# Last batch of a Fourier stage: spectra kept in SBUF, its inverse blocks moved, logits in groups of six and two batches

## The chip, the cores and the metric

One core of a Trainium2 chip. The metric is the device time of one launch in microseconds (us), as the median of three runs. A 0.2% difference is 2.9 us.

## What is computed

Two layers in a row. The first is a filter in the frequency domain, the second a mixture of experts with a greedy, global assignment of tokens:

```python
X = np.fft.rfft(x, axis=1)                 # x: 8 batches x 2496 x 256, float32
y = np.fft.irfft(X * (filt_r + 1j * filt_i)[None], n=2496, axis=1)
t = y.reshape(19968, 256)
logits = t @ w_gate                        # 19968 x 8
order = np.argsort(-logits.flatten())      # best pairs first
# go through order: a token takes its expert unless it has one, or the expert has 2496 already
for e in range(8):
    out[mask_e] = np.maximum(t[mask_e] @ w1[e], 0) @ w2[e]
```

## The kernel before

The length 2496 is taken as 39 x 64, and the program has three stages on one core.

**Fourier stage** (`Fft.run`). It is written as a table of events; each has a slot (ten slots a batch) and a priority, and a scheduler then lays the instructions of each engine in one fixed order. For a batch b the steps are: `s1` (first transform), `s2` (second transform, ten blocks of TensorE matmuls; DVE multiplies each with the filter F into P and Q, POOL combines them; the ten results P are the batch's spectra), `tr` (ten blocks q: four transposes of spectra into PSUM, then `split` into a high part yh on ACT and a low part yl on DVE), `inv1` (first inverse transform of block q: six matmuls over two rows of 256, a copy of PSUM into a tile zt, and two DMA stores of zt, 128 KB each, into the HBM buffer zd of the batch). zt has four buffers (ZB). `inv2` is the second inverse transform: a unit loads 600 KB of zd as a tile z, and its rows go to xs in HBM.

The logits don't wait for the inverse transform. They are computed from the spectra: gate matmuls on P (in `tr`), a transpose (`trv`) with a split into Vh and Vl, `v1` (an inverse transform for the logits alone, five groups g), a copy of its result on ACT, `v2` (22 transposes and a copy), `v3` (a matmul and a copy into lg), and `Route.prep` (seven DVE instructions over lg). Batches 0 to 6 go through v1, v2, v3 and prep together, batch 7 alone behind them. When its prep is done, the first round of the expert threshold starts.

**Routing and the remaining units** (`emit`). 30 units of inv2 remain when the logits are done. They are woven by hand, in one TensorE order, with the eleven threshold rounds (`Route.threshold`; a round is eleven to thirteen count matmuls `rt<-A,Gm` of L569, a few short DVE steps, one matmul L582, a few DVE steps). Blocks q = 0 and 1 of batch 7 stand among its own steps, q = 2 to 4 right behind its v3, and q = 5 to 9 between the first parts of units. For q > 4 (in `tr`) the transposed spectra are copied to SBUF, and their split is done later, its low part on POOL.

**Experts** (`Ffn`). They begin when all of xs has been written: L1004 on POOL waits for the last unit's copy, then weights and tokens are gathered.

Two things order DMAs. DMAs are issued by SP or by ACT, each in its own program order; and each DMA counts on one of eight semaphores in turn, so that it is issued after the one eight before it has landed. In this kernel the stores of zt go out on SP for batches 0 to 5 and on ACT for 6 and 7 (L307). When the last s2 block is done, SP loads six units into the freed tiles cW and F (`more_z`, L374), and when v1 is done two more into Vh and Vl.

Of the kernel before, what the change touches and what calls it, by code (L numbers as in the profile page):

```python
# [15 lines left out]
G = 22  # L16
S = B * G
# [112 lines left out]
class Fft:  # L130


    def __init__(s, tc, i, xs, zd, lg, pp):
        s.tc, s.nc, s.i, s.xs, s.zd, s.lg, s.pp = tc, tc.nc, i, xs, zd, lg, pp
        s.zw = s.zo = s.y7 = s.y9 = None
# [97 lines left out]
    def s2(s, b, g, dh):  # L233

        nc = s.nc
        p = s.ps.tile([128, 4, 128], F32, name="p2", tag="b", bufs=2)
        for k in range(4):
            nc.tensor.matmul(p[:, k], s.Y1[b][:, 4*g+k, dh*128:dh*128+128], s.cW[:, 4*g+k], start=True, stop=True)  # L238
        P = s.yt[b, g, dh] = s.wp.tile([128, 4, 128], F32, name="P", bufs=NP)
# [9 lines left out]
    def tr(s, b, q):  # L249

        nc = s.nc
        g, k = q // 2, 2 * (q % 2)
        yt = [s.yt[b, g, dh] for dh in range(2)]
        p = s.ps.tile([128, 2, D], F32, name="pa", tag="c", bufs=4)
        for h in range(2):
            for dh in range(2):
                nc.tensor.transpose(p[:, h, 128*dh:128*dh+128], yt[dh][:, k+h], s.id)
        if b == B - 1 and q > 4:
            nc.scalar.copy(s.y7b(q), p)
        else:  # L260
            s.split(b, q, p, nc.vector)
        if k:
            p = s.ps.tile([128, 128], F32, name="pv", tag="c", bufs=4)
            for dh in range(2):
                for k in range(4):
                    nc.tensor.matmul(p[32*k:32*k+32], s.gate[:, dh], yt[dh][:, k], start=dh == 0, stop=dh == 1, skip_group_check=True)
            s.vs[b, g] = s.wp.tile([128, 128], F32, name="vs", bufs=1)
            nc.scalar.copy(s.vs[b, g], p)

    def y7b(s, q):  # L270
        if q == 9 and s.y9 is None:
            s.y9 = s.wp.tile([128, 4, 128], F32, name="P", bufs=NP).rearrange("p k d -> p (k d)")
        y = s.y7[:, 80+512*q:592+512*q] if q < 9 else s.y9
        return y.rearrange("p (k d) -> p k d", d=D)
# [20 lines left out]
    def inv1(s, b, q):  # L295

        nc = s.nc
        if (b, q) not in s.yd:
            s.split(b, q, s.y7b(q), nc.gpsimd)
        zt = s.wp.tile([128, 2, D], F32, name="zt", bufs=ZB)  # L300
        p = s.ps.tile([128, 2, D], F32, name="pa", tag="c", bufs=4)
        for h in range(2):
            s.inv(p[:, h], 2*q + h, [y[:, h] for y in s.yd[b, q]])
        last = b == B - 1
        (nc.scalar.copy if last else s.cps[q % 2])(zt, p)
        for r in range(2):
            (nc.scalar if b >= B - 2 else nc.sync).dma_start(s.zd[b].rearrange("a n c -> n a c")[:N2, 20*r+2*q:20*r+2*q+2], zt[64*r:64*r+64])  # L307

    def pt(s, shape, fill):

# [2 lines left out]
    def v1(s, g, b0, b1):  # L313

        nc = s.nc
        if s.y7 is None:
            s.y7 = s.wp.tile([128, K1 * D], F32, name="Y1", tag="Y1", bufs=2)
            nc.gpsimd.memset(s.y7[:72, :2640].rearrange("p (a n) -> p a n", n=3*G)[:, :, N2:], 0.0)
        c = 8 * (b1 - b0)
        r = slice(64, 64 + c) if b0 else slice(0, c)  # L320
        p = s.pt([128, 4, 128], not b0)
        for k in range(4):
            (h, l), (Eh, El) = ([t[:, 4*g+k] for t in ts] for ts in ((s.Vh, s.Vl), s.cE))
            for m, (v, w) in enumerate(((h, Eh), (h, El), (l, Eh))):
                nc.tensor.matmul(p[:c, k], v[:, 8*b0:8*b1], w, start=m == 0, stop=m == 2)
        z = s.y7[r, :2640].rearrange("p (r k n) -> p k r n", r=2, k=K1)[:, 4*g:4*g+4, :, :N2]
        nc.scalar.copy(z, p[:c].rearrange("p k (r n) -> p k r n", r=2))

    def v2(s, b0, b1):

# [76 lines left out]
    def run(s, cp, wp, xp, ps, freed, prep, rest):  # L407
# [13 lines left out]
        for b in range(B):  # L421
# [23 lines left out]
        at(10*B - V2, 3.8, s.v2, 0, B - 1)
        def prep0():
            with s.tc.issue_after(s.lastq):
                prep(0, G * (B - 1))
        at(10*B - 0.9, 3.7, s.v3, 0, B - 1)
        at(10*B - VP, 3.8, prep0)  # L450
# [21 lines left out]
class Route:  # L472
# [75 lines left out]
    def counts(s, nj, thr, made=False):  # L548
# [374 lines left out]
def emit(tc, i, out):  # L923
    nc = tc.nc
    with ExitStack() as st:
# [206 lines left out]
```

## Time and profile before

| | |
|---|---|
| median of three runs | 1441.48 us (1440.28 to 1443.21) |
| profiled execution | 1455.17 us |
| its span | 1453.3 us, 27296 instructions |
| PE busy | 1388.1 us (96%) |
| mean granted TensorE clock | 0.985 |

The profiled execution is 13.7 us longer than the median; the span is what the trace holds of it, and 1.9 us lie around it. Times in the trace count from the span's start. Engines: PE is TensorE, PEld its weight loads, DVE, ACT, POOL and SP the others; L327 is line 327 of the kernel before.

### The profile page before, as it was taken

The page shows a single profiled execution, that of the slowest core. Times are in us where ns is not written, and L with a number is a line of the kernel's source. Part 1 is how long each engine was busy: PE and PEld are TensorE (multiplying, and loading weights), DVE is VectorE, ACT ScalarE, POOL GpSimd, SP SyncE. Part 2 cuts the span into 40 slices and gives each one's busy share as a digit, 9 for nine tenths or more (in the row PEclk, how much of TensorE's full clock was granted, in tenths as well). Part 3 has the DMA queues.
Part 4 walks back from the last instruction along what each step waited for, and adds up shares of the span by engine and source line. Part 5 has one row for each costly group of instructions (what it writes and reads, how often), then busy time and mean ns, then how long its engine had stood idle before and what let it go on. Part 6 is the DMA issues. An engine that isn't in the chain of part 4 may idle for free. (4 is left out here: it accounts for less than half of the span.)

```text
span 1453.3 us, 27296 instructions
## 1 busy us (share of the span) xinstructions
PE 1388.1 (96%) x10338; PEld 1215.1 (84%) x10338; DVE 898.1 (62%) x2568; ACT 679.2 (47%) x1658; POOL 485.4 (33%) x538
## 2 busy tenths in 40 slices
PE   8799999998968999999899999999999999999998
PEld 8698888986436888888798888889898898899988
DVE  6476677676546777667766877777866735333231
ACT  7576666644464236325424534533632635433232
POOL 3343334441013215413422542443414333333212
PEclk9899999999988999999999999999999999999999
DMA  9977775558882103102212112111201321111100
GB/s 244 245 200 200 205 200 139 141 135 220 324 318 77 35 26 106 53 21 95 61 35 81 51 51 85 52 47 39 102 26 53 129 70 48 42 46 50 39 23 28
DMA packets 57992, 150.66 MB, mean 104 GB/s; under 512 B 10999, under 2 KB 32247, under 8 KB 54409
## 3 DMA queue, kind: packets, MB, share of 16 engines
q1 hardware_dynamic: 29068, 66.86, 17.3%
q0 software_dynamic: 18416, 60.37, 12.8%
q10 hardware_dynamic: 10377, 21.68, 4.5%
q8 instruction: 82, 1.34, 0.4%
q14 instruction: 49, 0.40, 0.1%
HBM read 85.23 MB, written 63.70 MB: 102 GB/s over the span
## 5 line engine op out<-in xcount | busy, mean ns | idle before, releaser
L901 PE MATMUL py<-w1h,hl 128*128 128x256 f32 x2496 | 485.4, 287 | 1.7 <-DVE hl L869 0.7
L901 PEld LDWEIGHTS py<-w1h,hl 128*128 128x128 f32 x2496 | 402.1, 191 | 8.5 <-issue 4.5
L901 PE MATMUL py<-w1l,hl 128*128 128x256 f32 (+1 forms) x1280 | 359.2, 283 | 0.4 <-issue 0.4
L912 POOL DMA_INDIRECT out<-y,oid x160 | 168.9, 1056 | 516.3 <-ACT y L911 467.0
L864 ACT ACTIVATE hl<-pz 128x512 fp32r<-128x512 f32 (+1 forms) x320 | 187.2, 587 | 228.9 <-PE pz L858 191.6
L858 PE MATMUL pz<-xo,w0h 128*128 128x512 f32 (+1 forms) x640 | 264.8, 414 | 4.0 <-DVE hl L866 1.9
L866 DVE SCALAR_TENSOR_TENSOR hl<-pz,hl 128x512 fp32r<-128x512 f32 x256 | 175.1, 688 | 144.0 <-ACT hl L864 127.6
L858 PE MATMUL pz<-z,w0h 128*128 128x512 f32 (+1 forms) x640 | 249.0, 389 | 0.4 <-DVE z L840 0.4
L858 PE MATMUL pz<-xo,w0l 128*128 128x512 f32 (+1 forms) x640 | 249.3, 389 | 0.0
L901 PEld LDWEIGHTS py<-w1l,hl 128*128 128x128 f32 (+1 forms) x1280 | 241.1, 188 | 2.7 <-issue 0.7
L822 POOL DMA_INDIRECT xg<-xs,xid x160 | 168.5, 1053 | 137.0 <-issue 54.8
L911 ACT COPY y<-py 128x256 f32<-128x256 f32 x152 | 56.6, 372 | 313.1 <-PE py L901 253.9
L858 PEld LDWEIGHTS pz<-xo,w0h 128*128 128x128 f32 x640 | 121.9, 191 | 23.2 <-DVE hl L866 3.0
L858 PEld LDWEIGHTS pz<-xo,w0l 128*128 128x128 f32 x640 | 121.0, 189 | 24.0
L858 PEld LDWEIGHTS pz<-z,w0h 128*128 128x128 f32 x640 | 121.9, 191 | 16.6 <-DVE z L840 1.3
L226 ACT COPY Y<-p 64x240 f32<-64x240 f32 (+1 forms) x302 | 115.3, 382 | 25.1 <-PE p L220 17.8
L246 POOL TENSOR_TENSOR P<-P 128x256 f32<-128x256 f32 x80 | 59.0, 737 | 182.2 <-DVE P L244 182.1
L561 DVE TENSOR_TENSOR Gm<-M,thr 117x1232 bf16<-117x1232 f32 (+2 forms) x80 | 104.4, 1315 | 0.2
L220 PE MATMUL p<-cS,xr 117*128 117x120 f32 x688 | 95.6, 278 | 8.1 <-DMA xr<-x 6.0
L220 PEld LDWEIGHTS p<-cS,xr 117*128 117x128 f32 x688 | 86.8, 194 | 12.5 <-issue 7.4
L238 PE MATMUL p<-cW,Y 128*128 128x128 f32 x640 | 89.6, 277 | 0.6 <-DVE Q L245 0.6
L238 PEld LDWEIGHTS p<-cW,Y 128*128 128x128 f32 x640 | 80.6, 191 | 6.0 <-issue 4.1
(220 smaller groups left out, 2010.2 us busy)
## 6 DMA issues: line engine op xcount, KB each, us to landing
z<-zd SPq DMA_DIRECT2D x26, 600.0 KB
zd<-zt SPq DMA_DIRECT2D x120, 128.0 KB
xs<-xo ACTq DMA_DIRECT2D x18, 600.0 KB
xr<-x SPq DMA_DIRECT2D x6, 1344.0 KB
xr<-x SPq DMA_DIRECT2D x6, 1064.0 KB
zd<-zt ACTq DMA_DIRECT2D x40, 128.0 KB
xs<-xo SPq DMA_DIRECT2D x8, 600.0 KB
xs<-Y ACTq DMA_DIRECT2D x6, 600.0 KB
```

Source lines behind the costliest of these rows:

```text
L220: s.lastmm = nc.tensor.matmul(p[:, q-q0, :120], xv[:, q-24*h], s.cS1, start=True, stop=True).ins
L226: c = (nc.vector.tensor_copy if (t == 5 if b else cp) else nc.scalar.copy)(dst, src)
L238: nc.tensor.matmul(p[:, k], s.Y1[b][:, 4*g+k, dh*128:dh*128+128], s.cW[:, 4*g+k], start=True, stop=True)
L246: nc.gpsimd.tensor_tensor(P[:, :, :64], P[:, :, :64], P[:, :, 64:], op=OP.subtract)
L561: nc.vector.tensor_tensor(Gm[:, s0:s1, :m], s.M[:, s0:s1].unsqueeze(2).to_broadcast([117, s1 - s0, m]), thr[:117].unsqueeze(1).to_broadcas ...
L822: s.lastg = s.nc.gpsimd.indirect_dma_start(out=xg[:n], out_offset=None, in_=s.xs, in_offset=bass.IndirectOffsetOnAxis(ap=ids[0][:n, t:t+1] ...
L858: nc.tensor.matmul(p[:, :n], w[:, sl], x[:, k, :n], start=m == 0, stop=m == 5)
L864: s.lasta = nc.scalar.activation(h[:, :n], p[:, :n], AF.Relu).ins
L866: s.R.low = nc.vector.scalar_tensor_tensor(l[:, :n], p[:, :n], 0.0, h[:, :n].bitcast(F32), op0=OP.max, op1=OP.subtract).ins
L901: nc.tensor.matmul(p[:a.stop-a.start], hs[g][f][:, a], b[:, 256*f:256*f+256], start=m == 0, stop=m == 8 * len(terms) - 1, skip_group_check ...
L911: s.lasta = nc.scalar.copy(y, p).ins
L912: st = nc.gpsimd.indirect_dma_start(out=out_rows, out_offset=bass.IndirectOffsetOnAxis(ap=ids[1][:w, 4*g+t:4*g+t+1], axis=0), in_=y[:w], i ...
```

## The change

Batch 7's ten spectra are all kept: four in the tile y7 (which has the buffer of Y1), five in the P tiles, and the last in one of the four zt buffers. Its gate matmuls become a function of their own (`gates`) and come right behind its s2 blocks; its `tr` and `inv1` come later, q = 0 to 6 (QT = 7) among the steps of its logits and q = 7 to 9 among the first units, where a tr now stands right before its inv1. All of its splits are tr's own, with the low part on DVE. The logits go in groups of batches 0 to 5 and 6 to 7. The copies of v3 are on ACT for the first group. The first part of a unit is issued behind the counts of round 0. And batch 7's stores of zt go out on SP.

```diff
@@ s2
+        j = 2*g + dh if b == B - 1 else 4
+        if j < 4:
...
+            P = s.y7[:, 2640+512*j:3152+512*j].rearrange("p (k d) -> p k d", k=4)
+        elif j < 9:
+            P = s.wp.tile([128, 4, 128], F32, name="P", bufs=NP)
+        else:
+            P = s.wp.tile([128, 2, D], F32, name="zt", bufs=ZB).rearrange("p h (k d) -> p (h k) d", k=2)
@@ tr
-        if b == B - 1 and q > 4:
-            nc.scalar.copy(s.y7b(q), p)
+        with s.tc.issue_after(s.lastq) if b == B - 1 else nullcontext():
+            s.split(b, q, p, nc.vector)
+        if k and b < B - 1:
+            s.gates(b, g)
@@ inv1
-            (nc.scalar if b >= B - 2 else nc.sync).dma_start(s.zd[b]...
+            (nc.scalar if b == B - 2 else nc.sync).dma_start(s.zd[b]...
@@ run
-            at(10*B - V1 + g*V1D, 3.8, s.v1, g, 0, B - 1)
-            at(10*B - 5.2 + 2*g, 3.6, s.v1, g, B - 1, B)
+            at(10*B - V1 + g*V1D, 3.8, s.v1, g, 0, B - 2)
+            at(10*B - 7 + 2*g, 1.6, s.v1, g, B - 2, B)
...
-        for q in (2, 3, 4):
-            at(10*B + 2.9, 3.7 + 0.01 * q, s.inv1, B - 1, q)
+        for q in range(QT):
+            at(10*B - 0.9 + 0.3*q, 5, s.tr, B - 1, q, "a")
+            at(10*B - 0.35 + 0.3*q, 5, s.inv1, B - 1, q, "b")
@@ emit
-            q = 5
+            q = QT
...
                     if q < 10:
+                        f.tr(B - 1, q)
+                        yield 0.9
                         f.inv1(B - 1, q)
...
+        with tc.issue_after(R.lastc):
+            next(units)
```

What this makes of the order is seen at three places. First SP, where the loads of `more_z` and `more_z2` (into cW, F, Vh, Vl; the lines of inv1's stores are L307 and L316) stand. Before:

```order
L374 DMA cW<-zd_64 120x1280 x2
L374 DMA F<-zd_63 120x1280 x2
L374 DMA F<-zd_63 120x512
L374 DMA F<-zd_64 120x1280
L374 DMA Vh<-zd_64 120x1280
L374 DMA Vl<-zd_64 120x512
L374 DMA z<-zd_65 120x1280 x4
```

Now:

```order
L379 DMA cW<-zd_64 120x1280 x2
L379 DMA F<-zd_63 120x1280 x2
L379 DMA F<-zd_63 120x512
L379 DMA F<-zd_64 120x1280
L316 DMA zd_67<-zt 64x2x256 x6
L379 DMA Vh<-zd_64 120x1280
L379 DMA Vl<-zd_64 120x512
L316 DMA zd_67<-zt 64x2x256 x12
L379 DMA z<-zd_65 120x1280
L316 DMA zd_67<-zt 64x2x256 x2
```

The twenty stores of batch 7, before on ACT, stand here now, the first six (q = 0, 1, 2) behind the six loads into cW and F. Second ACT, from the copy of the logits' fourth group on (L327 and L333 are v1's copies into Y, L305 and L314 inv1's into zt, L278 and L289 the high parts). Before, the copy of the fifth and last group is the second L327:

```order
L327 COPY Y_3932<-pv 8x4x2x64
L268 COPY vs<-pv 128x128
L287 CAST Vh<-pv 128x4x8
L327 COPY Y_3932<-pv 8x4x2x64
L305 COPY zt<-pa 128x512
L278 CAST yh<-Y_3932 128x512
L307 DMA zd_67<-zt 64x2x256 x2
```

Now it is the last L333, and the copies into zt of q = 2 and q = 3 stand before it, those of q = 4 to 6 behind:

```order
L333 COPY Y_3753<-pv 16x4x2x64 x2
L285 COPY Y_3753<-pv 128x128
L314 COPY zt<-pa 128x512
L289 CAST yh<-pa 128x512 x2
L298 CAST Vh<-pv 128x4x8
L289 CAST yh<-pa 128x512
L314 COPY zt<-pa 128x512
L333 COPY Y_3753<-pv 16x4x2x64
L314 COPY zt<-pa 128x512 x3
```

Third PE, from the end of the second group's v1 to the first counts (L341 and L347 are v2, L351 and L357 v3, L293 and L304 inverse blocks, L569 and L575 the counts). Before, v2 and v3 came back to back and three inverse blocks stood between v3 and the counts:

```order
L325 MATMUL pv<-cEl,Vh 8x128
L325 MATMUL pv<-cEh,Vl 8x128
L341 MATMUL pv<-fid,Y_3932 120x8 x22
L351 MATMUL pv<-xo,cD 120x176
L293 MATMUL pa<-yh,cEh 128x256
```

Now one inverse block (q = 5) stands before v2, one (q = 6) between v2 and v3, and none behind v3:

```order
L304 MATMUL pa<-yh,cEl 128x256
L347 MATMUL pv<-fid,Y_3753 120x16 x22
L304 MATMUL pa<-yh,cEh 128x256
L304 MATMUL pa<-yl,cEh 128x256
L304 MATMUL pa<-yh,cEl 128x256
L304 MATMUL pa<-yh,cEh 128x256
L304 MATMUL pa<-yl,cEh 128x256
L304 MATMUL pa<-yh,cEl 128x256
L357 MATMUL pv<-xo,cD 120x352
L575 LDWEIGHTS Gm
```

Up to batch 7's first s2 blocks the order of every engine is what it was (the first group's v1 is 48 wide instead of 56), and from the first expert's matmuls on it is the same again.

## Rows read from the trace of the kernel before

**Rows 1.** The page, part 1: busy us, share of the span, instructions.

```profile
PE 1388.1 (96%) x10338; PEld 1215.1 (84%) x10338; DVE 898.1 (62%) x2568; ACT 679.2 (47%) x1658; POOL 485.4 (33%) x538
```

**Rows 2.** Windows: length, busy PE PEld DVE ACT POOL, PEclk, DMA share, GB/s.

```profile
322.00:326.00 4.00, 3.28 (x46) 2.67 (x44) 2.63 (x5) 2.10 (x5) 1.09 (x2) 1.00 0.90 211
326.00:330.00 4.00, 3.28 (x41) 2.41 (x40) 3.25 (x7) 2.11 (x6) 0.37 (x1) 1.00 0.97 230
330.00:334.00 4.00, 2.94 (x43) 1.96 (x41) 3.97 (x4) 2.38 (x6) 0.00 (x0) 1.00 0.94 222
334.00:338.00 4.00, 3.22 (x23) 3.13 (x24) 2.34 (x4) 0.29 (x1) 0.00 (x0) 0.95 1.00 246
338.00:340.00 2.00, 2.00 (x10) 2.00 (x11) 1.19 (x5) 0.01 (x1) 0.00 (x0) 0.50 0.88 213
340.00:342.00 2.00, 2.00 (x15) 1.86 (x15) 1.18 (x4) 1.21 (x3) 0.70 (x1) 0.75 0.28 78
```

**Rows 3.** Timeline of PE: start, us, instruction, idle before and its releaser.

```profile
320.24 1.05 PE L238 MATMUL p<-cW,Y 128*128 128x128 f32 x8
...
334.35 2.95 PE L341 MATMUL pv<-fid,Y 8*120 8x8 f32 x22 [0.67 <-ACT Y L327]
337.73 0.94 PE L351 MATMUL pv<-xo,cD 120*120 120x176 f32 x2 [0.43 <-DVE xo L342]
...
341.83 0.68 PE L569 MATMUL rt<-A,Gm 117*48 117x128 bf16 x9
```

**Rows 4.** Timeline of ACT and POOL: last logits copy; the wait before the experts.

```profile
333.72 0.57 ACT L327 COPY Y<-pv 8x512 f32<-8x512 f32 x1 [1.15 <-PE pv L325]
...
424.27 0.18 POOL L1004 COPY sidx<-xo 1x1 f32<-1x1 f32 x1 [73.38 <-ACT xo L401]
```

**Rows 5.** Timeline of DVE: a low part, copies into lg, first and last of prep.

```profile
323.26 0.69 DVE L279 TENSOR_TENSOR yl<-pa,yh 128x512 fp32r<-128x512 f32 x1 [2.30 <-ACT yh L278]
...
327.04 0.51 DVE L353 COPY lg<-pv 117x336 f32<-117x336 f32 x1 [0.53 <-PE pv L351]
...
338.71 0.34 DVE L353 COPY lg<-pv 117x176 f32<-117x176 f32 x1 [1.03 <-PE pv L351]
339.09 0.34 DVE L538 TENSOR_REDUCE M<-lg 117x22 f32<-117x176 f32 x1
...
340.94 0.34 DVE L545 TENSOR_TENSOR A<-ar,row 117x176 bf16<-117x176 f32 x1
```

**Rows 6.** Timeline of SP's queue, 320 to 348.

```profile
321.32 0.87 SPq L374 DMA_DIRECT2D cW<-zd  x2
325.38 1.68 SPq L374 DMA_DIRECT2D F<-zd  x4
333.65 0.32 SPq L374 DMA_DIRECT2D Vh<-zd  x1
```

**Rows 7.** Timelines of SP's queue and of DVE in an earlier stage, 54 to 70.

```profile
54.27 4.55 SPq L208 DMA_DIRECT2D xr<-x  x4
58.92 12.96 SPq L307 DMA_DIRECT2D zd<-zt  x10
...
69.93 0.69 DVE L305 COPY zt<-pa 128x512 f32<-128x512 f32 x1 [6.88 <-DMA zd<-zt]
```

**Rows 8.** Windows around a pause of PE, columns as in rows 2.

```profile
388.00:390.00 2.00, 0.32 (x1) 0.00 (x0) 0.28 (x2) 0.00 (x0) 0.00 (x0) 1.00 0.86 290
...
394.00:395.00 1.00, 1.00 (x3) 0.47 (x2) 0.78 (x2) 0.00 (x0) 0.00 (x0) 0.50 0.81 276
395.00:396.00 1.00, 1.00 (x3) 0.22 (x2) 0.00 (x0) 0.59 (x1) 0.00 (x0) 0.68 0.74 138
```

**Rows 9.** Timeline of PE, the matmul L582 of rounds 0, 1, 3 and 4.

```profile
345.78 0.17 PE L582 MATMUL rt<-X,ones 128*128 128x24 f16 x1 [1.09 <-DVE X L579]
...
351.85 0.20 PE L582 MATMUL rt<-X,ones 128*128 128x56 f16 x1
...
363.85 0.19 PE L582 MATMUL rt<-X,ones 128*128 128x56 f16 x1
...
368.92 0.19 PE L582 MATMUL rt<-X,ones 128*128 128x56 f16 x1
```

More of the change, by code (lines that the diff above doesn't have):

```diff
@@ L25 @@
 ORD, TF = (1, 0, 0, 1), (3, 5)
+QT = 7
 I1, C0 = 5, -2
@@ L134, in __init__ @@
         s.tc, s.nc, s.i, s.xs, s.zd, s.lg, s.pp = tc, tc.nc, i, xs, zd, lg, pp
-        s.zw = s.zo = s.y7 = s.y9 = None
+        s.zw = s.zo = s.y7 = None
         s.xos = []
@@ L238, in s2 @@
             nc.tensor.matmul(p[:, k], s.Y1[b][:, 4*g+k, dh*128:dh*128+128], s.cW[:, 4*g+k], start=True, stop=True)
-        P = s.yt[b, g, dh] = s.wp.tile([128, 4, 128], F32, name="P", bufs=NP)
+        j = 2*g + dh if b == B - 1 else 4
+        if j < 4:
+            if s.y7 is None:
+                s.y7 = s.wp.tile([128, K1 * D], F32, name="Y1", tag="Y1", bufs=2)
+                nc.gpsimd.memset(s.y7[:80, :2640].rearrange("p (a n) -> p a n", n=3*G)[:, :, N2:], 0.0)
+            P = s.y7[:, 2640+512*j:3152+512*j].rearrange("p (k d) -> p k d", k=4)
[3 more added lines that the diff above has]
+            P = s.wp.tile([128, 2, D], F32, name="zt", bufs=ZB).rearrange("p h (k d) -> p (h k) d", k=2)
+        s.yt[b, g, dh] = P
         Q = s.wp.tile([128, 4, 128], F32, name="Q", bufs=1)
@@ L247, in s2, with tr @@
         nc.gpsimd.tensor_tensor(P[:, :, 64:], Q[:, :, :64], Q[:, :, 64:], op=OP.add)
-    def tr(s, b, q):
+    def tr(s, b, q, tag="c"):
         nc = s.nc
@@ L253, in tr @@
         yt = [s.yt[b, g, dh] for dh in range(2)]
-        p = s.ps.tile([128, 2, D], F32, name="pa", tag="c", bufs=4)
+        p = s.ps.tile([128, 2, D], F32, name="pa", tag=tag, bufs=4 if tag == "c" else 2)
         for h in range(2):
@@ L257, in tr, with gates @@
                 nc.tensor.transpose(p[:, h, 128*dh:128*dh+128], yt[dh][:, k+h], s.id)
-        if b == B - 1 and q > 4:
-            nc.scalar.copy(s.y7b(q), p)
-        else:
[L261 to L274, printed above, removed]
+        with s.tc.issue_after(s.lastq) if b == B - 1 else nullcontext():
+            s.split(b, q, p, nc.vector)
+        if k and b < B - 1:
+            s.gates(b, g)
+    def gates(s, b, g):
+        nc = s.nc
+        p = s.ps.tile([128, 128], F32, name="pv", tag="c", bufs=4)
+        for dh in range(2):
+            for k in range(4):
+                nc.tensor.matmul(p[32*k:32*k+32], s.gate[:, dh], s.yt[b, g, dh][:, k], start=dh == 0, stop=dh == 1, skip_group_check=True)
+        if b < B - 1:
+            s.vs[b, g] = s.wp.tile([128, 128], F32, name="vs", bufs=1)
+        else:
+            s.vs[b, g] = s.y7[:, 4688+128*(g%3):4816+128*(g%3)]
+        nc.scalar.copy(s.vs[b, g], p)
     def split(s, b, q, v, eng):
@@ L293, in inv, with inv1 @@
             s.nc.tensor.matmul(p, w, v, start=m == 0, stop=m == 2)
-    def inv1(s, b, q):
+    def inv1(s, b, q, tag="c"):
         nc = s.nc
-        if (b, q) not in s.yd:
-            s.split(b, q, s.y7b(q), nc.gpsimd)
         zt = s.wp.tile([128, 2, D], F32, name="zt", bufs=ZB)
-        p = s.ps.tile([128, 2, D], F32, name="pa", tag="c", bufs=4)
+        p = s.ps.tile([128, 2, D], F32, name="pa", tag=tag, bufs=4 if tag == "c" else 2)
         for h in range(2):
@@ L306, in inv1 @@
         for r in range(2):
-            (nc.scalar if b >= B - 2 else nc.sync).dma_start(s.zd[b].rearrange("a n c -> n a c")[:N2, 20*r+2*q:20*r+2*q+2], zt[64*r:64*r+64])
+            (nc.scalar if b == B - 2 else nc.sync).dma_start(s.zd[b].rearrange("a n c -> n a c")[:N2, 20*r+2*q:20*r+2*q+2], zt[64*r:64*r+64])
     def pt(s, shape, fill):
@@ L315, in v1 @@
         nc = s.nc
-        if s.y7 is None:
-            s.y7 = s.wp.tile([128, K1 * D], F32, name="Y1", tag="Y1", bufs=2)
-            nc.gpsimd.memset(s.y7[:72, :2640].rearrange("p (a n) -> p a n", n=3*G)[:, :, N2:], 0.0)
         c = 8 * (b1 - b0)
@@ L333, in v2 @@
         s.U = s.zp.tile([120, G, c], F32, name="xo", tag="xo", bufs=2)
-        n = 8 if c > 8 else G
+        n = 8 if c > 16 else G
         for g0 in range(0, G, n):
@@ L346, in v3 @@
         nc, c = s.nc, 8 * (b1 - b0)
-        n = 8 if c > 8 else G
+        n = 8 if c > 16 else G
         for g0 in range(0, G, n):
@@ L351, in v3 @@
             s.lastv = nc.tensor.matmul(p[:120], s.cD, s.U[:, g0:g1], start=True, stop=True).ins
-            with s.tc.issue_after(s.lastq):
-                nc.vector.tensor_copy(s.lg[:, b0:b1, g0:g1], p[:117].rearrange("p g (b e) -> p b g e", e=8))
+            (nc.vector.tensor_copy if b0 else nc.scalar.copy)(s.lg[:, b0:b1, g0:g1], p[:117].rearrange("p g (b e) -> p b g e", e=8))
     def more_z(s, units):
@@ L430, in run @@
                     at(o + 2*g + dh, 1, s.s2, b, g, dh)
-                at(o + 2*g + 4.5, 3.5, s.trv, b, g)
-            for q in range(10):
+                if b < B - 1:
+                    at(o + 2*g + 4.5, 3.5, s.trv, b, g)
+                else:
+                    at(o + 2*g + 2.1, 1.5, s.gates, b, g)
+                    at(o + 2*g + 2.6, 1.5, s.trv, b, g)
+            for q in range(10 if b < B - 1 else 0):
                 at(o + q + 3, 3, s.tr, b, q)
-                if b < B - 1 or q < 2:
-                    at(o + q + I1, 4, s.inv1, b, q)
+                at(o + q + I1, 4, s.inv1, b, q)
             for t in range(5):
@@ L442, in run @@
         for g in range(5):
-            at(10*B - V1 + g*V1D, 3.8, s.v1, g, 0, B - 1)
-            at(10*B - 5.2 + 2*g, 3.6, s.v1, g, B - 1, B)
[L445 to L450, printed above, removed]
+            at(10*B - V1 + g*V1D, 3.8, s.v1, g, 0, B - 2)
+            at(10*B - 7 + 2*g, 1.6, s.v1, g, B - 2, B)
+        at(10*B - 4.2, 3.8, s.v2, 0, B - 2)
+        at(10*B - 3.6, 3.8, s.v3, 0, B - 2)
+        at(10*B - 3, 3.8, prep, 0, G * (B - 2))
         def act():
@@ L457, in run @@
         at(10*B + 2.9, 3.61, s.more_z2, rest[9+NZ:3+NZ+MZ])
-        at(10*B + 2.9, 3.6, s.v2, B - 1, B)
-        at(10*B + 2.9, 3.62, s.v3, B - 1, B)
-        at(10*B + 2.9, 3.64, prep, S - G, S)
-        for q in (2, 3, 4):
-            at(10*B + 2.9, 3.7 + 0.01 * q, s.inv1, B - 1, q)
+        at(10*B + 1.2, 3.6, s.v2, B - 2, B)
+        at(10*B + 1.2, 3.62, s.v3, B - 2, B)
+        at(10*B + 1.2, 3.64, prep, S - 2*G, S)
+        for q in range(QT):
+            at(10*B - 0.9 + 0.3*q, 5, s.tr, B - 1, q, "a")
+            at(10*B - 0.35 + 0.3*q, 5, s.inv1, B - 1, q, "b")
         for e in sorted(ev, key=lambda e: e[:3]):
@@ L568, in counts @@
             w = min(b, S - b*k) * n
-            nc.tensor.matmul(c[:KL, :w], s.Gm[:, K*k:K*k+KL], s.A[:, b*n*k:b*n*k+w], start=k == 0, stop=k == last, skip_group_check=True)
+            s.lastc = nc.tensor.matmul(c[:KL, :w], s.Gm[:, K*k:K*k+KL], s.A[:, b*n*k:b*n*k+w], start=k == 0, stop=k == last, skip_group_check=True).ins
         t1 = s.wp.tile([128, 128], F32, name="t1", bufs=2)[:K, :b*n].rearrange("p (e s) -> p e s", s=b)
```

## The prediction, made before the changed kernel was run

> **What bounds the kernel now.** I read the page first: PE is busy for 96% of the span [rows 1], so time can be won or lost only where PE stands still, runs at the low clock, or is held by a chain. The order of instructions is the same from the first expert's matmuls on; whatever the change is worth is therefore a shift of the moment at which the experts can start, and that moment is the last unit's copy into xs, on which POOL waits until 424.27 [rows 4]. Back from there, the units and the eleven threshold rounds are woven in one fixed order on PE, so they start together, with the first counts (L569) at 341.83 [rows 3]. The question is when these counts start in the changed kernel, and how fast the first rounds go.
>
> What the counts wait for is read in the windows and timelines before them. From 322 to 338 PE is busy for 3.28, 3.28, 2.94 and 3.22 us of 4 each, and then runs 2.0 us at a granted clock of 0.50, the lower of its two levels (1.2 GHz) [rows 2]: about 3.3 us of idle and 1 to 1.5 us of slow clock lie here. The chain at its end is: last copy of v1 on ACT at 333.72 [rows 4], v2 on PE from 334.35 for 2.95 us, v3 at 337.73 [rows 3], the copy into lg at 338.71 and prep until 341.28 (340.94 + 0.34) [rows 5], counts at 341.83. From the end of that ACT copy (334.29) to the counts it is 7.54 us. Beside it, the 16 DMA engines are 0.88 to 1.00 busy from 322 to 340 and then drop to 0.28 [rows 2]: these are the loads into cW, F and Vh [rows 6].
>
> **The change part by part.**
>
> *PE's work* stays the same. By the order, between a point common to both and the counts there are 12 transposes fewer and 12 inverse matmuls more, and behind it 12 transposes more and 12 inverse matmuls fewer; at some 0.13 us for a transpose (22 in 2.95 us [rows 3]) and about as much for the others this is nothing, here or there. So the gain could only be the 4 to 5 us of idle and slow clock above, filled by seven tr and inv1 blocks.
>
> *Stores on SP behind the loads.* The store of q = 0 now stands on SP behind two loads into cW and four into F. The cW loads are issued when the last s2 block has left PE, 320.24 + 1.05 = 321.3 [rows 3], and were, at 321.32 [rows 6]. The PE work ahead of that point changes by less than a microsecond, so I take 321.3 again. The six loads hold five times 600 KB and 240 KB, 3.32 MB. The windows from 322 moved 0.84, 0.92, 0.89 and 0.98 MB [rows 2], 3.64 MB by 338; if the loads are served in turn, six are through at about 336.7, and at the latest at 340, where the DMA share falls. I take 337.5. What a store does behind loads of the same queue is to be seen at 58.92 [rows 7]: SP issued ten stores of zt behind four loads of x (begun at 54.27), and the DVE copy that needed one of the tiles back stood 6.88 us, until 69.93, for "DMA zd<-zt". So q = 0's two stores (0.26 MB, 1.1 us at 240 GB/s) land at about 338.6; bounds 337.5 and 341.
>
> The Trainium skill, "DMA: Bandwidth & Descriptors", section "Issuing engines are not separate DMA queues", says that DMAs of all issuers run on the same 16 engines and interleave, and that the choice of issuer saves only its issue time. By that alone a store on SP would land as one on ACT did, ACT would not stop, and the sum would be about 1442.9 (second rival); rows 7 show a store held up behind its own queue's loads, which stands against it.
>
> *Who waits for these stores.* Of the four zt buffers one now holds the last spectrum until the tr of q = 9, behind the counts. So q = 0, 1, 2 take the other three, and the copy of q = 3 needs q = 0's tile back. That copy stands on ACT directly before the last copy of v1 (L333), and ACT takes its instructions in order. Behind it on PE are the inverse block of q = 5, which needs q = 3's PSUM buffer (two of tag b), then v2, v3 and all counts. ACT gets there at about 332 to 333, when it would have made the last v1 copy anyway, and stands until 338.6. Then 0.6 us for the zt copy (0.69 on DVE [rows 7]) and 0.57 for L333 [rows 4]: it ends at 339.8 against 334.29, **+5.5 us** (bounds +4.4 and +7.9).
>
> *From there to the counts.* The second group is now two batches wide: the copy into lg and five steps of prep go from 176 to 352 elements, 0.34 to 0.51 us by the 336-element copy [rows 5], the copy of v2's result likewise, and v3 has twice the columns: 7 times 0.17 and 0.2, **+1.4 us**.
>
> *Clock.* PE stands still from about 333 to 339.5. After a pause in which PE was busy for 0.32 of 2 us, the level was 0.50 from 394 to 395 and back only in the next microsecond (mean 0.68) [rows 8]. At 1.2 GHz the 2.95 us of v2 [rows 3] take up to twice as long; between nothing and +3 I take **+1.5 us**.
>
> *First rounds.* Each of q = 7, 8, 9 now has tr and inv1 back to back on PE. inv1 must wait for yh on ACT and then yl on DVE (0.69 us [rows 5]), and DVE has yl behind the round's own steps; the round's L582 or counts stand on PE behind that inv1. That is up to 0.7 to 0.8 us for each, +2.3 at most. Against it, ACT no longer issues stores among the units' copies. Rounds 2 and 3 took 12.0 us together (351.85 to 363.85) where a round later takes 5.07 (363.85 to 368.92) [rows 9]; if they reach that pace, 1.9 us come back. I take **0**, bounds -1.9 and +2.3. The rest of the window is unchanged in order and paced by PE; I cost it at nothing, and if its cover of DMA were gone it would show as ACT waiting for stores into xs.
>
> Sum: 5.5 + 1.4 + 1.5 + 0 = +8.4 us. The profiled execution would take 1455.17 + 8.4 = 1463.6; on the median, 13.7 us below it, 1441.5 + 8.4 = **1449.9 us**. With the bounds of the four terms added, 1445 to 1456.
>
> **The rivals.**
>
> *Faster: the blocks fill PE and nothing stops.* If q = 0's stores land before ACT needs the tile (before about 332, so six loads and a store in 11 us, some 325 GB/s where the windows show 211 to 246 [rows 2]), or if something else lets the chain run early, the idle and slow clock go: -3.3 and -1.3, with +1.4 for the wider group and -1.9 in rounds 2 and 3 this is -5.1, 1436.4 us. For it speaks that the gate matmuls now follow s2 at once and that the DVE, which stood 2.30 us for a yh at 323.26 [rows 5], has no split before its last filter products.
>
> *Same: no stop, but nothing won.* The stores interleave with the loads instead of following them and come in time, but the last v1 copy comes where it did, since it ends a chain of gate, copy, transpose, split and v1 that PE's filling doesn't shorten. Then +1.4 of wider prep and rounds near 0: 1442.9. For it speaks that behind v3 no PE work is left to lay beside prep, against it the 6.88 us [rows 7]. By the Trainium skill's section named above it would go this way.
>
> *Much slower: the low clock stays.* PE stops a second time, for about 4 us while prep runs, and rounds 0 and 1 go at 1.2 GHz too. Then the clock term is 4 to 6 us, with loads through only at 340 the sum is 1456 to 1458. This is the upper end of the forecast, with the same sign.
>
> **How the numbers follow.** The forecast with its upper end gets 66% (of which 8% above 1455), no stop without gain 17%, the faster one 17%. A measurement of this kernel can tell about 0.2%, 2.9 us: faster means under 1438.6, slower over 1444.4. The same rival lies within, so: faster 0.17, same 0.17, slower 0.66. The time is that of the likeliest, 1449.9, its own range 1445 to 1456. For 8 in 10 I leave out half of the faster case (below 1437.5) and the 8% above 1455.
>
> **What the profile will show.** If right: in ACT's timeline a copy L314 into zt idle for some 5 us with "DMA zd<-zt" as releaser, shortly before the last L333; v2 (L347) starting near 340 and the first counts (L575) near 350, with a granted clock of 0.5 between; cW and F loads near 321 to 324 as before. Units, rounds 4 to 10 and experts then follow at the old distances. If the waits on zt are short and the counts come at 342 or sooner, the step on the queue is wrong; if they are there and the end is not later, rounds 0 to 3 have given back more than 1.9 us, and that step is.

## The result, and the profile after

The changed kernel takes 1452.09 us (median of five, 1451.31 to 1459.62), the kernel before 1440.28 (median of five). The ratio is 1.0087, 95% interval 1.0061 to 1.0113: 12 us slower. The profiled execution of the changed kernel is the 1459.62, 7.5 us above its median, so its landmarks are read for the mechanism, and sizes are taken from ratios.

The page, part 1, of the changed kernel: PE does the same 10338 instructions as in [rows 1].

```profile
PE 1394.3 (96%) x10338; PEld 1220.7 (84%) x10338; DVE 899.5 (62%) x2570; ACT 680.2 (47%) x1656; POOL 480.0 (33%) x533
```

The windows that answer to [rows 2], with the same columns.

```profile
326.00:330.00 4.00, 3.85 (x47) 3.41 (x47) 4.00 (x8) 2.86 (x6) 0.48 (x1) 1.00 0.97 235
330.00:334.00 4.00, 3.80 (x36) 3.29 (x34) 2.55 (x4) 2.52 (x6) 0.00 (x0) 1.00 0.97 236
334.00:338.00 4.00, 1.79 (x21) 1.59 (x20) 1.48 (x3) 0.65 (x2) 0.00 (x0) 1.00 0.98 242
338.00:340.00 2.00, 0.00 (x0) 0.00 (x0) 0.00 (x0) 0.00 (x0) 0.00 (x0) 0.87 0.96 277
340.00:342.00 2.00, 0.10 (x1) 0.11 (x1) 0.00 (x0) 0.72 (x2) 0.00 (x0) 0.50 1.04 344
342.00:348.00 6.00, 6.00 (x35) 5.74 (x36) 0.53 (x1) 1.61 (x3) 0.00 (x0) 0.50 0.81 215
348.00:354.00 6.00, 2.98 (x15) 1.60 (x14) 4.01 (x10) 0.59 (x1) 0.00 (x0) 0.78 0.19 44
354.00:360.00 6.00, 4.97 (x19) 2.54 (x17) 2.12 (x10) 2.17 (x4) 0.00 (x0) 0.79 0.00 0
```

The moved blocks do fill PE from 326 to 334, 7.65 us of 8 against 6.22. Then PE and the other compute engines stand while DMA is 0.96 to 1.04 busy: from 334 to 342 PE is busy for 1.89 us, before for 7.22. It starts again at the lower clock, stops a second time from 350 to 353, and DMA falls to nothing. ACT's and SP's timelines name the first stop.

```profile
335.11 0.59 ACT L289 CAST yh<-pa 128x512 fp32r<-128x512 f32 x1 [1.05 <-PE pa L268]
341.26 0.59 ACT L314 COPY zt<-pa 128x512 f32<-128x512 f32 x1 [5.56 <-DMA zd<-zt]
341.87 0.58 ACT L333 COPY Y<-pv 16x512 f32<-16x512 f32 x1
```

```profile
323.24 0.77 SPq L379 DMA_DIRECT2D cW<-zd  x2
325.49 1.68 SPq L379 DMA_DIRECT2D F<-zd  x4
327.85 10.46 SPq L316 DMA_DIRECT2D zd<-zt  x6
```

The copy of q = 3 waits 5.56 us for q = 0's stores, which SP issues behind six loads, and the last v1 copy stands behind it. PE's timeline: v2, v3, the first counts (eleven, in two pieces, the second behind prep), then round 0 and the matmul of rounds 0, 1, 2 and 10.

```profile
322.32 0.88 PE L239 MATMUL p<-cW,Y 128*128 128x128 f32 x6
...
343.48 2.96 PE L347 MATMUL pv<-fid,Y 16*120 16x16 f32 x22
...
347.81 1.38 PE L357 MATMUL pv<-xo,cD 120*120 120x352 f32 x2
349.12 0.89 PE L575 MATMUL rt<-A,Gm 117*48 117x128 bf16 x8
353.04 0.43 PE L575 MATMUL rt<-A,Gm 117*48 117x128 bf16 x3 [3.02 <-DVE A L551]
353.39 2.06 PE L405 MATMUL pv<-z,cD 120*120 120x512 f32 x2
...
358.41 0.19 PE L588 MATMUL rt<-X,ones 128*128 128x24 f16 x1
...
360.71 0.38 PE L304 MATMUL pa<-yh,cEh 128*128 128x256 f32 x1 [0.72 <-ACT yh L289]
362.20 0.39 PE L304 MATMUL pa<-yl,cEh 128*128 128x256 f32 x1 [1.11 <-DVE yl L290]
...
368.31 0.27 PE L588 MATMUL rt<-X,ones 128*128 128x56 f16 x1
...
373.89 0.19 PE L588 MATMUL rt<-X,ones 128*128 128x56 f16 x1
...
415.33 0.20 PE L588 MATMUL rt<-X,ones 128*128 128x72 f16 x1
```

And POOL's wait before the experts, 17.1 us later than in [rows 4].

```profile
441.38 0.18 POOL L1014 COPY sidx<-xo 1x1 f32<-1x1 f32 x1 [114.90 <-ACT xo L406]
```

The table gives these landmarks for all kernels, in us from the end of the last s2 matmul (start plus duration of the last L239 or L238; 322.32 + 0.88 here). The rest of a run follows sidx as a block: q3_behind, late_loads, tr_first and comb1, on one chip, end 1013.5 to 1013.8 us behind it. Between chips and executions that rest differs by more (1016.5 us in pool_stores on that same chip, 1029.0 in the profiled execution of before, 1016.2 in that of after), so times are compared by the ratio to the kernel before on the same chip, the last column. A difference of two ratios, given below in us, is uncertain by 4 to 5 us.

| kernel | s2 end | v2 | round 0 | round 2 | round 10 | sidx | ratio (95%) |
|---|---|---|---|---|---|---|---|
| before | 321.29 | 13.1 | 24.5 | 36.9 | 81.8 | 103.0 | 1 |
| after | 323.20 | 20.3 | 35.2 | 50.7 | 92.1 | 118.2 | 1.0087 (1.0061-1.0113) |
| act_stores | 320.62 | 21.3 | 36.2 | 51.8 | 93.2 | 119.9 | 1.0091 (1.0070-1.0112) |
| three_act | 320.05 | 20.4 | 35.3 | 51.0 | 92.7 | 117.6 | 1.0079 (1.0056-1.0102) |
| seven_one | 317.83 | 21.1 | 34.5 | 50.1 | 91.6 | 114.0 | 1.0050 (1.0027-1.0073) |
| before_sp | 318.89 | 13.1 | 23.9 | 37.7 | 82.4 | 103.6 | 1.0015 (1.0001-1.0029) |
| q3_behind | 321.10 | 12.6 | 26.5 | 41.5 | 82.9 | 108.6 | 1.0025 (1.0011-1.0039) |
| late_loads | 322.49 | 14.2 | 31.9 | 49.1 | 90.7 | 114.6 | 1.0068 (1.0048-1.0088) |
| tr_first | 321.87 | 20.5 | 34.7 | 45.6 | 89.7 | 112.7 | 1.0055 (1.0036-1.0075) |
| comb1 | 320.60 | 13.8 | 25.8 | 37.0 | 81.4 | 102.7 | 0.9998 (0.9982-1.0014) |
| best_act | 322.03 | 13.8 | 25.5 | 36.8 | 80.4 | 101.7 | 0.9975 (0.9955-0.9996) |
| best_unit | 321.80 | 15.3 | 27.8 | 39.6 | 82.0 | 104.6 | 1.0008 (0.9985-1.0031) |
| best_both | 321.23 | 15.2 | 27.7 | 40.6 | 82.7 | 104.3 | 0.9984 (0.9961-1.0008) |
| pool_stores | 319.44 | 16.0 | 31.6 | 47.1 | 89.1 | 113.0 | 1.0081 (1.0058-1.0103) |

The end of s2 itself differs by up to 5.4 us, mostly for reasons that are not the change's. From the first matmul of batch 7's s2 to the last it is 27.35 us before (293.94 to 321.29), and 26.55 in act_stores, three_act, q3_behind, tr_first and pool_stores, all at a granted clock of 1.00: with the changed kernel's order s2 ends 0.8 us sooner, not later. In the profiled execution of the changed kernel it began 1.1 us later, at 295.03, and took 28.17 us at a clock of 0.94; the first windows of that stretch, before and after, show where.

```profile
294.00:298.00 4.00, 4.00 (x44) 4.00 (x44) 3.31 (x10) 1.61 (x5) 1.50 (x3) 1.00 0.95 234
294.00:298.00 4.00, 3.79 (x21) 3.79 (x22) 2.01 (x10) 0.91 (x3) 0.65 (x3) 0.64 0.97 250
```

### The profile page after: what moved, and what is told of

Same layout as the page of the kernel before. It is cut to its first block, busy times and chain, and to the rows that moved or that the text cites. A ratio compares the mean times of both kernels' runs of the same rounds, so it can differ in the third digit from the quotient of the medians.

```text
span 1457.6 us, 27299 instructions
## 1 busy us (share of the span) xinstructions
PE 1394.3 (96%) x10338; PEld 1220.7 (84%) x10338; DVE 899.5 (62%) x2570; ACT 680.2 (47%) x1656; POOL 480.0 (33%) x533
## 5 line engine op out<-in xcount | busy, mean ns | idle before, releaser
L227 ACT COPY Y<-p 64x240 f32<-64x240 f32 (+1 forms) x302 | 115.3, 382 | 25.0 <-PE p L221 18.1
L257 POOL TENSOR_TENSOR P<-P 128x256 f32<-128x256 f32 x75 | 55.3, 737 | 172.3 <-DVE P L255 172.2
L239 PE MATMUL p<-cW,Y 128*128 128x128 f32 x640 | 92.0, 282 | 0.6 <-DVE Q L256 0.6
L239 PEld LDWEIGHTS p<-cW,Y 128*128 128x128 f32 x640 | 82.7, 196 | 6.1 <-issue 4.0
```

Source lines behind the costliest of these rows:

```text
L227: c = (nc.vector.tensor_copy if (t == 5 if b else cp) else nc.scalar.copy)(dst, src)
```

## The experiments

My theory was the prediction's: the stores' queue makes the stop, the stop makes the loss. The rivals were that the issuer does not matter, that the wider group or the first rounds cost it, and that DMA sets the end.

**The issuer.** Three kernels change one line, the one that says who issues stores. In act_stores and three_act the scheduler then lays the orders a little differently too: on ACT the copy into zt of q = 4 also stands before the last v1 copy. Their edit, in `inv1` of the changed kernel:

```diff
-(nc.scalar if b == B - 2 else nc.sync).dma_start(
+(nc.scalar if b >= B - 2 else nc.sync).dma_start(                      # act_stores
+(nc.scalar if b == B - 2 or last and q < 3 else nc.sync).dma_start(   # three_act
```

> The changed kernel with batch 7's stores of zt issued by ACT again, nothing else. Theory Q (the stores stand on SP behind six loads, so the tile of q = 0 comes back late): the wait "DMA zd<-zt" of 5.56 us on ACT falls below 1 us, v2 (L347) starts at 335 to 338 instead of 343.48, the first counts at 342 to 345, and the time falls from 1452.1 to 1441-1446. Rival I (DMAs of all issuers interleave, so the issuer changes only issue time, and the loss comes from the wider group and the blocks behind the counts): the wait stays at 4 us or more and the time at 1450-1454.

> The changed kernel with only the stores of q = 0, 1, 2 (those behind the six loads) on ACT; those of q = 3 to 9 stay on SP. Theory Q with the wait for q = 0's tile as the whole loss: same as with all on ACT within 2 us. Theory Q2 (the stores on SP also hold back SP's z loads behind them, which started at 348 before and at 365 after): the wait is gone, but z loads still start at 355 or later, DMA is idle around 350-358 again, and the time is 3 to 7 us above the version with all on ACT, 1445-1450. Rival I: 1450-1454.

In act_stores the wait on zt is nearly gone (0.99 us, and that is q = 4's copy), but the loss is not: v2 comes 21.3 us after s2, as late as ever. ACT's timeline of act_stores shows why.

```profile
332.01 4.78 ACTq L316 DMA_DIRECT2D zd<-zt  x2
336.89 0.59 ACT L289 CAST yh<-pa 128x512 fp32r<-128x512 f32 x1 [5.80 <-DMA F<-zd]
...
339.68 0.59 ACT L314 COPY zt<-pa 128x512 f32<-128x512 f32 x1 [0.99 <-DMA zd<-zt]
340.29 0.57 ACT L333 COPY Y<-pv 16x512 f32<-16x512 f32 x1
```

ACT stands 4.78 us at the issue of two stores, and its next cast is released by a load into F: SP and ACT share the eight semaphores, and a store on ACT may be issued only when the DMA eight before it has landed. The stop moves from a copy to an issue, on the same engine, ahead of the same v1 copy. Theory Q's forecast for act_stores failed; three_act came within 2 us of it, as forecast, but with the loss still there. Rival I had the time right and the wait wrong. The addition to Q, that stores on SP hold back SP's z loads, fell too: in act_stores the z loads begin at 362.96 with no store of batch 7 on SP, since they wait 16.7 us for the first units' matmuls (L405).

before_sp makes the same move alone, on the kernel before (`b == B - 2` in place of `b >= B - 2`).

> The kernel before with batch 7's stores of zt on SP, nothing else. By the order the stores of q = 0 and 1 stand ahead of the loads into cW and F here, and all four zt buffers are there. If the issuer matters only through the missing buffer: within 2 us of the kernel before. Theory Q2 (stores on SP hold back the z loads, whose start falls from 348 to 355 or later): 3 to 8 us slower. Rival I: within 1 us.

It costs 2 us (1.0015, 1.0001 to 1.0029); v2 comes at its old distance of 13.1. Where no store is needed back early, the queue is close to nothing.

**The wider group.** seven_one puts the groups back.

```diff
-at(10*B - V1 + g*V1D, 3.8, s.v1, g, 0, B - 2)
-at(10*B - 7 + 2*g, 1.6, s.v1, g, B - 2, B)
+at(10*B - V1 + g*V1D, 3.8, s.v1, g, 0, B - 1)
+at(10*B - 7 + 2*g, 1.6, s.v1, g, B - 1, B)
...
```

> The changed kernel with the logits again in groups of batches 0 to 6 and 7 alone; the rest is as changed. Theory Q: the wait on zt stays at 4 to 6 us, v2, prep and the copies give back about 1.4 us (2 at the low clock), 1449.5-1451.5. Rival G (the wider group is what costs): prep and v2 come early, 1441-1446. Rival I without G: 1450-1452.

1.0050, 5.3 us better than the changed kernel (difference of the ratios times 1441), between the two forecasts and hardly more than its uncertainty. The wait is still 6.71 us and v2 as late after s2. From the first to the last matmul of batch 7's s2 it is 25.35 us, against 26.55 in the two above on the same chip, all at a clock of 1.00: with the wider group v1, v2 and v3 stand 1.2 us longer among the last s2 blocks. With prep's 1.2 us (below) this is less than half of the 5.3; most of what is left lies behind round 10, where PE's clock is 1.00 against 0.87 in act_stores and 0.93 in three_act.

**The place.** q3_behind issues the inverse blocks q = 3 to 6 behind v3, with the transposes of q = 6 (`inv1_late` is inv1 issued after v3's last matmul; the kernel's later lines move by four). late_loads leaves the blocks and issues the six loads behind q = 2's stores.

```diff
-at(10*B - 0.9 + 0.3*q, 5, s.tr, B - 1, q, "a")
-at(10*B - 0.35 + 0.3*q, 5, s.inv1, B - 1, q, "b")
+at(10*B - 0.9 + 0.3*q if q < 6 else 10*B + 1.2, 5 if q < 6 else 3.735, s.tr, B - 1, q, "a")
+at(10*B - 0.35 + 0.3*q if q < 3 else 10*B + 1.2, 5 if q < 3 else 3.7 + 0.01*q,
+   s.inv1 if q < 3 else s.inv1_late, B - 1, q, "b")            # q3_behind
...
-for u, z in zip(units, zs):
-    s.load_z(*u, z)
+with s.tc.issue_after(s.st.ins):
+    for u, z in zip(units, zs): s.load_z(*u, z)                 # late_loads
...
-at(10*B - 0.8, 9, s.more_z, rest[3+NZ:9+NZ])
+at(10*B + 0.3, 9, s.more_z, rest[3+NZ:9+NZ])
```

> The changed kernel with the inverse blocks of q = 3 to 6 issued behind v3 (q = 0 to 2 stay where they are), so that no copy into a zt tile that is still being stored stands on ACT in front of v1's last copy; stores on SP as changed. Theory S (the place of the blocks makes the stop, by whichever issuer the stores go): the copy of q = 3 may still wait for its tile, but behind the last v1 copy; v2 starts 5 to 7 us earlier than in the changed kernel, less than 16 us after the last s2 block, against 20.3, and the time is 5 to 8 us above the kernel before instead of 12.7 (ratio 1.0035 to 1.0055). Rival F (the end of the units is set by DMA or by the blocks among the first rounds, whenever the counts start): v2 earlier, but the time still 11 to 13 us above, 1.0075 to 1.009.

> The changed kernel with the six loads into cW and F issued on SP behind the stores of q = 0, 1 and 2 instead of ahead of them. Theory S: q = 0's stores land within 3 us, the wait "DMA zd<-zt" falls below 1 us, v2 starts less than 16 us after the last s2 block, and the time is 5 to 8 us above the kernel before. Rival F (DMA feeds the units, and every us in which it stands idle comes back at the end): the wait is gone too, but the loads start 7 to 10 us later, so that the units end no earlier than in the changed kernel: 12 us above or more, ratio 1.008 to 1.013.

q3_behind is 1.0025, 8.9 us better than the changed kernel and better than theory S's 1.0035 to 1.0055, with the stores on SP as changed. ACT, PE and the windows:

```profile
333.06 0.57 ACT L337 COPY Y<-pv 16x512 f32<-16x512 f32 x1 [1.70 <-PE pv L335]
340.12 0.59 ACT L314 COPY zt<-pa 128x512 f32<-128x512 f32 x1 [6.48 <-PE pa L304]
```

```profile
333.69 2.97 PE L351 MATMUL pv<-fid,Y 16*120 16x16 f32 x22 [0.67 <-ACT Y L337]
...
343.57 0.35 PE L579 MATMUL rt<-A,Gm 117*48 117x128 bf16 x3
```

```profile
338.00:340.00 2.00, 2.00 (x9) 1.74 (x8) 1.09 (x3) 0.00 (x0) 0.00 (x0) 0.50 1.07 364
340.00:342.00 2.00, 2.00 (x16) 1.68 (x14) 1.97 (x5) 1.66 (x3) 0.00 (x0) 0.62 0.91 218
342.00:348.00 6.00, 4.86 (x30) 3.55 (x30) 2.63 (x8) 2.28 (x5) 0.00 (x0) 1.00 0.82 203
```

The last v1 copy now starts at 333.06. The copy of q = 3 comes behind it and waits for PE, not for its tile; of the waits on zt one of 0.99 us is left, at 344.59. PE works on the moved blocks while DVE makes prep: from v2 to the last counts of round 0 it is 9.9 us (333.69 to 343.57) with four inverse blocks done on the way, against 9.6 (343.48 to 353.04) with one in the changed kernel. The clock is 1.00 from 342 to 348.

late_loads has v2 at 14.2 us, nearly as soon, and yet 1.0068, between the two forecasts. The wait is only carried on: ACT's next zt copy, of q = 6, needs q = 3's tile, whose stores now stand behind the loads, and the first unit's copies stand behind it.

```profile
350.76 0.59 ACT L314 COPY zt<-pa 128x512 f32<-128x512 f32 x1 [14.25 <-DMA zd<-zt]
351.24 0.59 ACT L406 COPY xo<-pv 120x512 f32<-120x512 f32 x1
```

**The first rounds.** tr_first makes the transposes of q = 7, 8 and 9 ahead of the first of their inverse blocks.

```diff
+if q == QT:
+    for qq in range(QT, min(QT + 3, 10)):
+        f.tr(B - 1, qq)
+        yield 0.5
 if q < 10:
-    f.tr(B - 1, q)
-    yield 0.9
+    if q > QT + 2:
+        f.tr(B - 1, q)
+        yield 0.9
```

> The changed kernel with the transposes and splits of q = 7, 8 and 9 all ahead of the first of their inverse blocks among the units, so that no inverse block waits for its own split. If tr directly before inv1 is what the first rounds lose by: the matmul L588 of round 2 comes 12 to 13 us behind that of round 0 instead of 15.5, the time 9 to 11 us above the kernel before (ratio 1.006 to 1.0075). Rival: the three low parts on DVE delay round 0's own steps as much, 12 to 13 us above (1.0083 to 1.009).

Rounds 0 to 2 take 10.9 us against 15.5, and 12.4 before; 1.0055, 4.6 us better than the changed kernel, both a little better than forecast. The rival's delay by three low parts did not come. The windows of these rounds, in the changed kernel and in tr_first, show that not only the waits went:

```profile
358.41:373.89 15.48, 12.81 (x60) 7.96 (x59) 7.86 (x24) 5.82 (x11) 0.00 (x0) 0.78 0.55 141
356.57:367.48 10.91, 9.70 (x62) 6.46 (x59) 7.67 (x24) 5.73 (x12) 0.00 (x0) 1.00 0.63 156
```

PE's idle time falls by 1.5 us, from 2.67 to 1.21; the other 3.1 are busy time, and the granted clock is 1.00 instead of 0.78.

**All three, and from there.** comb1 is q3_behind, seven_one and tr_first together.

> The changed kernel with three edits at once: inverse blocks of q = 3 to 6 behind v3, logits in groups of batches 0 to 6 and 7, and the transposes of q = 7 to 9 ahead of their inverse blocks. If the three losses add up (stop about 6 us, wider group 4 to 5, first rounds 2 to 3) this is the kernel before within 3 us: ratio 0.998 to 1.002. If they cover one another (the end is set by DMA, rival F): 1.004 to 1.008.

0.9998: the loss is gone, and no landmark differs from the kernel before by more than 1.3 us. Alone the three gave 8.9, 5.3 and 4.6 us, together 12.8, which suggests that they cover one another; with 4 to 5 us of uncertainty on each it is not shown. Three kernels add to it: best_act gives the stores of q = 3 to 9 to ACT (`or last and q > 2`), best_unit puts the first unit's three matmuls behind v1, best_both does both.

> The three edits of comb1, and the stores of q = 3 to 9 on ACT, so that SP's z loads have none of them ahead. In comb1 these loads begin at 351.94, against 348.07 in the kernel before. If the late z loads still cost there: they begin by 347 to 349 and the time is 1 to 3 us below the kernel before, ratio 0.998 to 0.9995. Rival: ACT now stands at the issue of these stores (4.78 us for two stores when all were on ACT) with the first units' copies behind, and the time is 1 to 4 us above, 1.0005 to 1.003.

> The three edits of comb1, and the first unit's three matmuls ahead of v2 on PE, where PE stands idle, its copies on ACT behind the last v1 copy, its store on SP. If PE's idle time ahead of the counts is worth filling: 1.3 us of work less behind them, and a clock that falls later, ratio 0.9975 to 0.9995. Rival: v2 starts 0.5 us later and the idle time is not where the units' end is decided: 0.9995 to 1.001.

> Both additions to comb1 together. If both gain, 0.996 to 0.999; if the stores on ACT cost, 1.000 to 1.003.

best_act is below both kernels, 0.9975 (0.9955 to 0.9996), but not by the step expected: its z loads begin at 353.18, not by 349. Why it is better than comb1, and by how much, stays open; the intervals overlap. best_unit's v2 starts at 15.3 us, 1.5 later than comb1's, and nothing came back, as its rival said. best_both, 0.9984, can't be told from comb1 or from best_act.

**The queue by itself.** In pool_stores POOL issues batch 7's stores (`nc.gpsimd if last`), with semaphores of its own. The orders of PE and ACT are those of the changed kernel, and so is DVE's up to the experts.

> The changed kernel with batch 7's stores of zt issued by POOL, which has nothing else to do there; its DMAs count on eight semaphores of their own, and the orders of PE, ACT and DVE are exactly those of the changed kernel. Theory Q (q = 0's stores are late because they must be issued behind the six loads, on SP by its order, on ACT by the eight semaphores that SP and ACT share; the blocks' place is harmless by itself): the wait "DMA zd<-zt" of 5.56 us falls below 1 us, v2 starts 14 to 16 us after the last s2 block instead of 20.3, SP's z loads begin by 352, and the time is 2 to 6 us above the kernel before, ratio 1.0015 to 1.004. Rival B (while the loads keep the 16 DMA engines 0.98 busy a store is late from any issuer): the wait stays at 3 us or more and the ratio at 1.006 to 1.009.

POOL's and ACT's timelines and the windows:

```profile
324.36 2.46 POOL L316 DMA_DIRECT2D zd<-zt  x4 [1.64 <-ACT zt L314]
```

```profile
333.94 0.59 ACT L314 COPY zt<-pa 128x512 f32<-128x512 f32 x1 [2.00 <-DMA zd<-zt]
334.55 0.58 ACT L333 COPY Y<-pv 16x512 f32<-16x512 f32 x1
```

```profile
342.00:348.00 6.00, 3.13 (x11) 1.70 (x9) 3.56 (x10) 0.46 (x2) 1.20 (x2) 0.50 0.21 44
348.00:354.00 6.00, 4.99 (x15) 2.84 (x13) 3.17 (x10) 2.05 (x5) 1.20 (x2) 0.54 0.11 22
```

SP had issued q = 0's stores as promptly (from 327.85, where q = 0's copy ended), so what held them there came after the issue, with six loads ahead of them in SP's queue. The DMA packets show it. In the changed kernel 105 of the 634 packets from 327.85 to 338 are smaller than 2 KB, as the stores' are and the loads' are not, and 812 of the 879 from 338 to 341.3. In pool_stores POOL's queue moves 0.75 MB from 330 to 335, while SP's moves 1.01. So POOL's stores go among the loads, and the wait falls from 5.56 to 2.00 us, between the two forecasts: v2 comes 4.2 us sooner, at 16.0, the end of theory Q's range. Theory Q's other two signs failed: the z loads begin at 357.20, not by 352, and the ratio is rival B's. Whether the time followed is open: 1.0081 can't be told from the changed kernel's 1.0087, while sidx comes 5.2 us sooner after s2 than in the changed kernel's profiled execution. From v2 to round 0 it is 15.5 us, against 11.4 before, and rounds 0 to 2 again take 15.5: nothing stands behind v3 to cover prep, PE is busy for half of 342 to 348, and the clock is 0.50 to 0.54 until 354. So the held stores are a part of the loss and not the whole of it.

## Why the prediction was right, step by step

- **The sign and the sum** came out: +11.8 us on the medians, forecast +8.4 with 1456 as upper end. The places were those named: a copy L314 idle 5.56 us for "DMA zd<-zt" ahead of the last L333 (forecast some 5), a clock of 0.50 between v2 and the counts, counts from 349.1 to 353.0 (forecast near 350). v2 came at 343.48, not near 340. Counted from the end of s2, the counts that need prep came 9.3 us later than before (353.04 - 323.20 against 341.83 - 321.29), where the terms ahead of them say 8.4, and sidx 15.2 us later. So some 6 us more lie behind the counts, where the forecast had 0, in this execution; that the time is inside the range is luck in this part.
- **PE work ahead of s2's end "changes by less than a microsecond"** holds: at the same clock the stretch is 26.55 us against 27.35. s2 ended 1.9 us later, at 323.20 against 321.29, since in this execution it began 1.1 us later and had the low clock. With it came the loads and the landing: the copy began at 341.26, just beyond the bound of 341, but within the bounds when counted from the end of s2 (18.1 us, forecast 17.3).
- **Stores on SP behind the loads** (+5.5, bounds 4.4 to 7.9): the mechanism is in the trace, and from s2's end to the end of the last L333 it is 19.2 us (342.45) against 13.0, +6.2. But SP was not what decided. On ACT the same stores hold ACT just as long through the shared semaphores (act_stores); only with POOL as issuer is the stop shorter. What made the stop is that a tile stored in the loads' time is needed back in front of the last v1 copy: with the blocks behind v3 no copy ahead of v2 waits for a tile (q3_behind). The Trainium skill, "DMA: Bandwidth & Descriptors", section "Issuing engines are not separate DMA queues", says that DMAs of all issuers interleave and the issuer saves only issue time. POOL's stores did land among SP's loads, but the same copy waited 5.56 us with SP as issuer and 2.00 with POOL, so here the issuer changed the landing too, and the measurement decides.
- **The wider group** (+1.4): from the copy into lg to the end of prep it is 3.75 us (349.23 to 352.98) against 2.57, +1.2 as worked out. The step counted only prep: the group also delays s2's end by 1.2 us (seven_one). The rest of seven_one's 5.3 us is within the uncertainty.
- **Clock** (+1.5): v2 itself was not longer, 2.96 us against 2.95, though at 0.50. What took its place ahead of the counts was costed at nothing: the inverse blocks of q = 5 and q = 6, at 0.50, hold v2 for 1.03 us behind the last L333 (before 0.06) and v3 for 1.37 us behind v2 (before 0.43). So from the end of L333 to the counts it is 10.6 us against 7.54, +3.1, where wider group and clock say +2.9: the sum fits, its parts do not. The low clock also cost behind prep, where the first unit's two matmuls took 2.06 us, and 1.10 at 358.45. This is the rival "the low clock stays" in part: PE stopped a second time, for 3.02 us (it said about 4). No run separates the clock from the uncovered prep.
- **First rounds** (0, bounds -1.9 to +2.3) was the term most mis-sized: rounds 0 to 2 took 15.5 us against 12.4, +3.1, and from the counts to round 0's matmul it is another 1.4. The waits named (yh on ACT, then yl on DVE, in front of inv1) are there, at 360.71 and 362.20 among others. But PE's idle time grew by 1.0 us only (1.70 to 2.67); the rest is busy time, at a granted clock of 0.78 against 1.00, which the step did not count. tr_first takes away both.
- **"Units, rounds 4 to 10 and experts follow at the old distances"** held only for the experts. Rounds 2 to 10 took 41.4 us against 45.0, and the rest to sidx 26.1 against 21.1, together +1.4. The windows from round 10's matmul to sidx, before and after, and PE's row in the second:

```profile
403.13:424.27 21.14, 18.24 (x58) 8.77 (x56) 11.64 (x77) 18.03 (x49) 0.00 (x0) 1.00 0.94 374
415.33:441.38 26.05, 21.91 (x60) 10.18 (x58) 12.48 (x84) 19.79 (x53) 0.00 (x1) 0.87 0.91 330
```

```profile
425.59 2.06 PE L405 MATMUL pv<-z,cD 120*120 120x512 f32 x2 [2.58 <-ACT xo L406]
```

Before, the stretch at the low clock lies among the rounds [rows 8]; in the changed kernel it lies behind round 10, where PE stopped for 2.58 us and then ran at 0.50 until about 431. So it reads as moved, not as new. In comb1 the clock behind round 10 is 1.00 again, and the rest takes 21.3 us.

The faster rival failed at the step that it named: the stores did not land before ACT needed the tile, and PE's filled 1.4 us (326 to 334) were lost in the stop behind them.

## What to carry to other kernels

Before work is moved into an idle stretch, ask what buffer it must get back in that stretch, and what stands behind that wait on its engine; here six DMA loads filled the stretch, and one copy of 0.6 us held the logits for 5.6. Ask too what the work had covered where it came from: blocks that kept PE busy beside a DVE chain were worth more there than in the gap. Where changing the issuer of a DMA doesn't move a stop, look at what the issue itself waits for before calling the queue innocent or guilty. And before a stage is called longer, compare its granted clock: batch 7's s2 took 28.2 us in one execution and 26.6 in others, in the same order.

## What was not expected of the hardware

- Two DMA issues on ACT held that engine for 4.78 us, released by loads that SP had issued.
- The 22 transposes of v2 did not follow the clock. Those of 8 x 8 took 2.95 us at a granted clock of 1.00 ([rows 3]) and 2.95 at 0.50 (seven_one), those of 16 x 16 2.96 at 0.50 (after).
- With the DMA engines 0.97 busy, q = 0's tile came back 9.6 us after POOL began to issue (324.36 to 333.94), and 13.4 us after SP did (327.85 to 341.26).
